# Gated linear attention and routed experts: first step in halves, decay rows turned as they land, sums of tiles 9 and 10 in two parts

## The chip, the cores and the metric

The kernel runs on one core of a Trainium2 chip. The core has TensorE for matrix products (PE; its weight loads are listed apart as PEld), VectorE (DVE), ScalarE (ACT) and GpSimd (POOL) for element work, and SyncE (SP), which here only issues transfers. ACT and POOL issue transfers of their own. The metric is the time of one execution in device microseconds.

## What is computed

A recurrent attention runs over 4 batches, 8 heads and 768 positions, with head dimension 48; its result, as 3072 rows of 384 numbers, goes through a layer of 8 experts, each row through the one expert that its gate prefers.

```python
for t in range(S):
    state = alpha[:, :, t, :, None] * state + einsum('bhd,bhe->bhde', k[:, :, t], v[:, :, t])
    y[:, :, t] = einsum('bhd,bhde->bhe', q[:, :, t], state)
x = y.transpose(0, 2, 1, 3).reshape(B * S, H * D)
logits = x @ w_gate                       # 3072 x 8
e = argmax(logits); gate_w = softmax(logits)[e]
out = gate_w * (relu(x @ w1[e]) @ w2[e])  # w1: 384 x 1024, w2: 1024 x 384
```

## The kernel before

The positions are cut into 6 chunks of 128, and a tile is one chunk of one batch: tile s is chunk c = s // 4 of batch b = s % 4, 24 tiles in all, chunk by chunk. Within a tile the recurrence becomes matrix products. The logarithms of alpha are summed over the positions by a product with a triangular matrix; the exponentials of the sum and of its negative (cp and icp) scale q and k; the scaled q and k are turned with the positions in columns, multiplied with each other (scores), masked by the triangle and multiplied with v. What earlier chunks left is a state for each head. It is scaled by a decay factor at each new chunk, and read by the scaled q.

One loop, over i from -4 to 23, does a step for each tile, with all stages shifted against each other. I call it step i. The order in which a step emits its operations is written out by hand (the pool of instructions is not reordered, L387), and so it is the order in each engine's queue. In step i:

- SP issues loads (`loads_for`, L629). Up to step 2 these are one tile of 192 KB each, in the order that the table `singly` (L623) spells out: "aakq" are two tiles of alpha, one of k and one of q. Later they go two tiles at a time.
- PE does the scores of tile i (L502), the turns of tile i+1 (L489), a sum (L430 or L433) of a tile up to five ahead, the reads of the state (L529, from tile 4 on), the products with v (`attend`, L539), in steps 0 to 2 a second sum, the products of keys and values for the state (`keys_values`, L550), and the rows of tile i-1 with their gate logits (L576).
- ACT copies y of tile i-1 out of its bank (yT, L558), takes an exponential for the gate (L590), the logarithm of alpha for the tiles whose sum is next (lna, L413), copies kT (L495), takes icp and cp (L436, L437), scales the finished rows (xs, L601) and issues the decay rows (L450).
- DVE applies the masks (dA, dB, L510), adds to the state (acc, L566 and L568), copies qT (L493, in early tiles also kT), and makes the gate weights.
- POOL makes the scaled k and q of tile i+2 (`operands`, L479) and the decayed state U (`scale_state`, L517), and in between prepares the routing.

A sum of tile s < APART = 11 is one product of f32 operands (L430). From tile 11 on the logarithm is split: hi is the logarithm times 512 in f16 (L418, on ACT), lo is the rest in a reduced f32 form (L423, on DVE), and the sum is two products (L432, L433). The hi and lo parts are made one step ahead of the sum. All sums use the PSUM bank "cum"; in steps below 0 the second sum uses the bank "x". In each step the sum waits until icp and cp of the sum before have read the bank.

The decay factor between two chunks of one batch is a product of three rows of 384: the last row of cp of the earlier chunk, the first row of icp of the later one, and alpha of the later one's first position. `decay_out` (L440) sends the first two as transfers from ACT's queue into a tile "dec" with one partition for each batch, and fetches alpha's rows for all four batches by one transfer from SP. `decay_rows` (L455) multiplies the three on POOL into "er", with every head padded from 48 to 64. `decay_cols` (L467) turns er by PE, four turns with 4 columns each, and copies the result to "E", which `scale_state` reads. decay_cols stands in steps 4, 8, 12, 16 and 20, behind the scores and ahead of the masks.

Ahead of the loop, `idle` (L637) issues three products on zeros from er, which DVE has set (L644). The layer of experts follows behind the loop. It is not touched.

## Time and profile before

| | us |
|---|---|
| median of three runs | 393.21 (391.83 to 393.31) |
| the profiled execution | 390.48 |
| its span, first to last instruction | 388.8 |
| attention loop, start to last mask | 0 to 133 |
| scores of step 0 start (PE's timeline) | 8.95 |
| scores of steps 1, 2, 3, 4, 5, 6 start | 14.08, 20.20, 26.07, 31.27, 37.05, 42.49 |
| granted TensorE clock, mean | 0.998 of full |
| transfers on queue q1 (SP's) | 57.77 MB, 63.2% of the transfer engines' time |
| transfers on queue q10 (ACT's) | 0.08 MB, 0.3% |

The profile is one execution. A line of a timeline holds the start in us, the duration in us, the engine, the line of the kernel, the operation, what it writes and reads, its shape and how many such operations were merged; in brackets stands how long the engine was idle before it and what it then waited for. ACTq and SPq are the issues of transfers in ACT's and SP's queue. In a list of waits, a line says which engine and line waited for which, the total in us, how often, and the longest wait. The durations of products on PE overlap one another, so from the start of one group to the start of the next is what a group costs.

### The profile page before, as it was taken

The page shows a single profiled execution, that of the slowest core. Times are in us where ns is not written, and L with a number is a line of the kernel's source. Part 1 is how long each engine was busy: PE and PEld are TensorE (multiplying, and loading weights), DVE is VectorE, ACT ScalarE, POOL GpSimd, SP SyncE. Part 2 cuts the span into 40 slices and gives each one's busy share as a digit, 9 for nine tenths or more (in the row PEclk, how much of TensorE's full clock was granted, in tenths as well). Part 3 has the DMA queues.
Part 4 walks back from the last instruction along what each step waited for, and adds up shares of the span by engine and source line. Part 5 has one row for each costly group of instructions (what it writes and reads, how often), then busy time and mean ns, then how long its engine had stood idle before and what let it go on. Part 6 is the DMA issues. An engine that isn't in the chain of part 4 may idle for free. (4 is left out here: it accounts for less than half of the span.)

```text
span 388.8 us, 9126 instructions
## 1 busy us (share of the span) xinstructions
PE 380.0 (98%) x3394; PEld 326.1 (84%) x3394; DVE 210.4 (54%) x649; ACT 230.2 (59%) x521; POOL 149.7 (39%) x203
## 2 busy tenths in 40 slices
PE   7999999999999999999999999999999999999995
PEld 4678888888888886899889979979979979979964
DVE  5554667676676666625843672582581582551200
ACT  4575777677665431545665775675765765763640
POOL 6557464789768203257050034025016012011032
PEclk9999999999999999999999999999999999999999
DMA  9999998998994315789959459758767966701211
GB/s 172 197 205 218 194 227 190 210 220 212 237 260 139 117 42 183 157 293 256 278 154 256 78 194 231 159 187 193 196 195 178 205 195 152 176 16 58 57 55 66
DMA packets 156546, 68.09 MB, mean 175 GB/s; under 512 B 139339, under 2 KB 150722, under 8 KB 156500
## 3 DMA queue, kind: packets, MB, share of 16 engines
q1 hardware_dynamic: 151396, 57.77, 63.2%
q0 software_dynamic: 3408, 9.64, 8.2%
q8 instruction: 28, 0.46, 0.5%
q10 hardware_dynamic: 1696, 0.08, 0.3%
q14 instruction: 18, 0.15, 0.1%
HBM read 49.00 MB, written 9.58 MB: 151 GB/s over the span
## 5 line engine op out<-in xcount | busy, mean ns | idle before, releaser
L1077 POOL DMA_INDIRECT out_dram<-zo,sp x25 | 26.0, 1041 | 136.5 <-ACT zo L1102 127.1
L479 POOL TENSOR_TENSOR kqb<-k_sb,icp 128x384 f32<-128x384 f32 x23 | 23.0, 1000 | 28.7 <-PE y L550 12.5
L1051 PE MATMUL tp<-h_sb,w 128*128 128x416 f32 (+5 forms) x96 | 33.9, 496 | 0.0
L502 PE MATMUL sA<-qT,kT 48*128 48x128 f32 x192 | 27.7, 284 | 0.9 <-DVE qT L493 0.9
L502 PE MATMUL sB<-qT,kT 48*128 48x128 f32 x192 | 27.7, 285 | 0.0
L372 POOL DMA_INDIRECT xg<-x_rows,gp x25 | 23.8, 953 | 10.0 <-issue 6.6
L489 PE MATMUL tp<-ident,kqb 128*128 128x128 f32 x192 | 26.4, 280 | 0.3 <-DVE kqb L479 0.3
L1051 PEld LDWEIGHTS tp<-h_sb,w 128*128 128x128 f32 x96 | 18.0, 190 | 10.3 <-issue 3.7
L502 PEld LDWEIGHTS sA<-qT,kT 48*128 48x128 f32 x192 | 23.1, 187 | 3.8 <-issue 1.1
L980 ACT ACTIVATE h_sb<-h_sb 128x208 f32<-128x208 f32 (+6 forms) x28 | 10.3, 366 | 25.3 <-DVE h_sb L192 24.5
L192 DVE TENSOR_TENSOR h_sb<-cum,u 128x208 f32<-128x208 f32 (+6 forms) x28 | 10.1, 360 | 27.2 <-PE cum L969 20.7
L479 POOL TENSOR_TENSOR kqb<-q_sb,cp 128x384 f32<-128x384 f32 x23 | 23.1, 1003 | 3.1 <-DMA q_sb<-in_q_dram 3.1
L192 DVE TENSOR_TENSOR h_sb<-sB,u 128x208 f32<-128x208 f32 (+6 forms) x28 | 10.1, 360 | 26.1 <-PE sB L969 18.7
L558 ACT COPY yT<-y 128x512 f32<-128x512 f32 x24 | 14.1, 586 | 16.5 <-PE y L550 9.1
L489 PEld LDWEIGHTS tp<-ident,kqb 128*128 128x128 f32 x192 | 20.5, 141 | 3.4 <-issue 0.8
L969 PE MATMUL tp<-xgT,w 128*128 128x208 f32 (+6 forms) x112 | 23.1, 329 | 0.0
L502 PEld LDWEIGHTS sB<-qT,kT 48*128 48x128 f32 x192 | 23.1, 187 | 0.0
L510 DVE TENSOR_TENSOR dA<-sA,cmask 128x512 f32<-128x512 f32 x24 | 16.5, 688 | 10.8 <-PE sB L502 10.6
L195 DVE TENSOR_TENSOR th<-h_sb,th 128x208 f32<-128x208 f32 (+5 forms) x48 | 17.3, 361 | 8.0 <-ACT h_sb L982 8.0
L881 ACT COPY xgT<-xt 128x768 uint16<-128x768 uint16 (+6 forms) x25 | 20.8, 922 | 0.5 <-DMA xt<-xh 0.5
L576 PE MATMUL x<-iw,yT 128*64 128x104 f32 x368 | 20.8, 255 | 0.1
L1102 ACT COPY zo<-zr 128x768 uint16<-128x768 uint16 (+2 forms) x20 | 19.9, 1052 | 0.0
(304 smaller groups left out, 1032.2 us busy)
## 6 DMA issues: line engine op xcount, KB each, us to landing
w<-in_moe_w_dram SPq DMA_DIRECT2D x14, 1536.0 KB, 7.9
x_rows<-xs SPq DMA_DIRECT2D x24, 192.0 KB, 3.7
v_sb<-in_v_dram SPq DMA_DIRECT2D x10, 384.0 KB, 4.8
k_sb<-in_k_dram SPq DMA_DIRECT2D x9, 384.0 KB, 6.3
q_sb<-in_q_dram SPq DMA_DIRECT2D x9, 384.0 KB, 5.9
a_sb<-in_alpha_dram SPq DMA_DIRECT2D x7, 384.0 KB, 4.3
a_sb<-in_alpha_dram SPq DMA_DIRECT2D x10, 192.0 KB, 3.7
w<-in_moe_w_dram SPq DMA_DIRECT2D x6, 256.0 KB, 3.7
```

What stands on the lines that cost most here:

```text
L192: eng.tensor_tensor(out, a, b, op=ALU.add)
L195: eng.tensor_tensor(out, a, b, op=ALU.subtract)
L372: nc.gpsimd.indirect_dma_start(out=g["xg"][:r, j, :], out_offset=None, in_=x_d[:, :], in_offset=bass.IndirectOffsetOnAxis(ap=g["gi"](j, r) ...
L479: eng.tensor_tensor(by_half(kq[:, i]), d[n].rearrange("s (a p) d -> s a p d", a=2), d[e][:].rearrange("s (a p d) -> s a p d", a=2, p=NP), ...
L489: nc.tensor.transpose(tp[:, p, :], pair(kqb[s % 3][:, i], p), ident[:])
L502: nc.tensor.matmul(t[:, p, :], lhsT=d["kT"][r : r + D, p, :], rhs=d["qT"][r : r + D, p, :], start=True, stop=True,)
L576: nc.tensor.matmul(d["x"][o : o + HC, m, : D2 + E], lhsT=d["yT"][:, m // 2, m % 2, o : o + HC], rhs=iw[:, m, :], start=True, stop=True,)
L881: nc.scalar.copy(to[:, :, :, j * C : j * C + r], g["xt"][:, j].rearrange("p (h a) t -> p h a t", h=2)[:, :, :, :r],)
L969: nc.tensor.matmul(out, lhsT=ops[n_][0], rhs=ops[n_][1], start=first and n_ == names[0], stop=True, skip_group_check=True,)
L1051: nc.tensor.matmul(d2[:, :n], lhsT=w2[:, f, 2 * C :], rhs=h[:, f, :n], start=(f == 0), stop=(f == FB - 1),)
L1077: ins = nc.gpsimd.indirect_dma_start(out=out[:, :], out_offset=bass.IndirectOffsetOnAxis(ap=g["si"](j, r), axis=0), in_=zo[:r], in_offset= ...
L1102: copy(zo[:r].bitcast(U16).rearrange("p (c h) -> p h c", h=2), g["zr"][:r, j].rearrange("p (h a) c -> p h (a c)", h=2),)
```

## The change

Four things are changed.

- *First step.* A function `first_step`, in step -2, replaces the sums of tiles 0 and 1, the operands of tile 0 (before on DVE in step -2) and its turns (before in step -1). The sum of tile 0 is made in two halves of two head pairs, in two banks; exponentials, operands, turns and copies go by halves. The sum of tile 1 stands between. In step 0 `keys_values` comes ahead of the second sum and no longer behind it. Two idle products of 512 columns on a constant zero stand ahead of everything, where three of 256 stood behind the first constants. In step -2 the load of v comes between the two of alpha.
- *Decay rows.* Three tiles "ends" of 20 partitions, filled with ones by POOL in step -4, take the rows as they are: for each chunk four rows of first positions of cp, four of last positions, four of alpha of the next chunk's first position (chunk 1 also those of chunk 0). Every head lands padded to 64. cp is stored with the heads in pairs, so that a row needs no other order. First and last row of a tile go in one transfer from ACT; alpha's rows go in two transfers from SP, and are asked for one chunk earlier. `decay_cols` turns all rows of the tile, takes the inverse of the first rows on the turned columns (the first row of cp in place of that of icp), multiplies it with what the chunk before handed on, and makes the product of last row and alpha to hand on.
- *Sums.* APART goes from 11 to 9, so tiles 9 and 10 are summed in two parts, and their logarithm and hi part are made one step earlier.
- `er`, `alpha0`, `decay_rows` and the "dec" tiles go.

```diff
@@ -65,7 +65,7 @@
     HC = C // 2
 
 
-    APART, HS = 11, 512.0
+    APART, HS = 9, 512.0
     assert NB * C == S and FB * C == F and DB * C == Dm and D <= DP
 
 
@@ -390,8 +390,8 @@
          tc.tile_pool(name="work", bufs=2) as work:
         st = {s: {} for s in range(NT)}
         y = ps.tile([C, 2, 512], F32, name="y")
-        er = work.tile([C, NP, 2, DP], F32, name="er", bufs=1)
-        decay, alpha0 = {}, {}
+        ends = [work.tile([5 * B, H, DP], F32, name=f"ends{i}", bufs=1) for i in range(3)]
+        decay, handed = {}, {}
 
         def yv(g):
             return y[:, g, : 2 * C].rearrange("r (j t) -> r j t", j=2)
@@ -424,8 +424,8 @@
                 t[:], in0=st[s]["hi"][:], scalar=-1.0 / HS, in1=st[s]["lna"][:], op0=ALU.mult, op1=ALU.add,
             )
 
-        def cums(s, bank="cum"):
-            cum = ps.tile([C, 512], F32, name="cum", tag=bank)
+        def cums(s):
+            cum = ps.tile([C, 512], F32, name="cum")
             if s < APART:
                 nc.tensor.matmul(cum[:, :Dm], lhsT=cum_m[:], rhs=st[s]["lna"][:], start=True, stop=True)
             else:
@@ -434,29 +434,32 @@
             cp = work.tile([C, Dm], F32, name="cp", bufs=6)
             icp = work.tile([C, Dm], F32, name="icp", bufs=6)
             nc.scalar.activation(icp[:], cum[:, :Dm], AF.Exp, scale=-1.0)
-            nc.scalar.activation(cp[:], cum[:, :Dm], AF.Exp)
+            nc.scalar.activation(by_pairs(cp), by_heads(cum[:, :Dm]), AF.Exp)
             st[s]["cp"], st[s]["icp"] = cp, icp
 
-        def decay_out(s, which=(0, 1)):
+        def decay_out(s):
+
+
             c, b = cb(s)
-            cp, icp = st[s]["cp"], st[s]["icp"]
-
-
-            for j in which:
-                cc, row = ((c, icp[0:1, :]), (c + 1, cp[C - 1 :, :]))[j]
-                if 0 < cc < NB:
-                    if cc not in decay:
-                        decay[cc] = work.tile([B, 2, Dm], F32, name="dec", bufs=3)
-                    nc.scalar.dma_start(decay[cc][b : b + 1, 1 - j, :], row)
-            if b == 0 and c + 1 < NB and 1 in which:
-                alpha0[c + 1] = work.tile([B, H, D], F32, name="alpha0", bufs=3)
-                nc.sync.dma_start(alpha0[c + 1][:], alpha[:, :, (c + 1) * C, :])
-
-        def decay_rows(c):
-            t = by_half(er[:B])
-            d = decay[c].rearrange("b i (a p d) -> b i a p d", a=2, p=NP)
-            nc.gpsimd.tensor_tensor(t, d[:, 0], d[:, 1], op=ALU.mult)
-            nc.gpsimd.tensor_tensor(t, t, alpha0[c].rearrange("b (a p) d -> b a p d", a=2), op=ALU.mult)
+            t = ends[max(c, 1) % 3]
+            first, last, alphas = (0, B, 2 * B) if c else (None, 3 * B, 4 * B)
+            if b == 0 and c + 1 < NB:
+                for a in range(2):
+                    nc.sync.dma_start(t[alphas : alphas + B, a::2, :D], alpha[:, a * NP : (a + 1) * NP, (c + 1) * C, :])
+            cp = st[s]["cp"].rearrange("s (h d) -> s h d", h=H)
+            if c == 0:
+                to, row = t[last + b : last + b + 1], cp[C - 1 :]
+            elif c + 1 < NB:
+                to, row = t[b : last + b + 1 : B], cp[:: C - 1]
+            else:
+                to, row = t[b : b + 1], cp[:1]
+            nc.scalar.dma_start(to[:, :, :D], row)
+
+        def by_heads(t):
+            return t.rearrange("s (a p d) -> s a p d", a=2, p=NP)
+
+        def by_pairs(t):
+            return t.rearrange("s (p a d) -> s a p d", a=2, p=NP)
 
         def by_half(t):
             return t.rearrange("s p a d -> s a p d")[:, :, :, :D]
@@ -465,21 +468,30 @@
             return t[:, p].rearrange("s a d -> s (a d)")
 
         def decay_cols(c):
+
+
+            n = 5 * B if c == 1 else 3 * B if c + 1 < NB else B
             ep = ps.tile([C, NP, C], F32, name="ep", tag="cum")
             for p in range(NP):
-                nc.tensor.transpose(ep[:, p, :B], pair(er[:B], p), ident[:B, :B])
+                nc.tensor.transpose(ep[:, p, :n], ends[c % 3][:n, 2 * p : 2 * p + 2, :].rearrange("r a d -> r (a d)"), ident[:n, :n])
             decay[c] = work.tile([C, NP, B], F32, name="E", bufs=2)
-            nc.vector.tensor_copy(decay[c][:], ep[:, :, :B])
+            nc.vector.reciprocal(decay[c][:], ep[:, :, :B])
+            if c == 1:
+                hand_on(c - 1, ep[:, :, 3 * B : n])
+            nc.vector.tensor_tensor(decay[c][:], decay[c][:], handed[c - 1][:], op=ALU.mult)
+            if c + 1 < NB:
+                hand_on(c, ep[:, :, B:n])
+
+        def hand_on(c, ep):
+            t = handed[c] = work.tile([C, NP, B], F32, name="handed", bufs=2)
+            nc.vector.tensor_copy(t[:], ep[:, :, :B])
+            nc.vector.tensor_tensor(t[:], t[:], ep[:, :, B : 2 * B], op=ALU.mult)
 
         def operands(s):
             d = st[s]
             kq = kqb[s % 3]
-            eng = nc.gpsimd if s else nc.vector
-            for i, n, e in ((0, "k", "icp"), (1, "q", "cp")):
-                eng.tensor_tensor(
-                    by_half(kq[:, i]), d[n].rearrange("s (a p) d -> s a p d", a=2),
-                    d[e][:].rearrange("s (a p d) -> s a p d", a=2, p=NP), op=ALU.mult,
-                )
+            for i, n, e in (0, "k", by_heads(d["icp"])), (1, "q", by_pairs(d["cp"])):
+                nc.gpsimd.tensor_tensor(by_half(kq[:, i]), d[n].rearrange("s (a p) d -> s a p d", a=2), e, op=ALU.mult)
 
         def transposes(s):
             d = st[s]
@@ -489,7 +501,7 @@
                     nc.tensor.transpose(tp[:, p, :], pair(kqb[s % 3][:, i], p), ident[:])
                 d[n] = work.tile([C, NP, C], F32, name=n)
 
-                if 0 < s < B - 1 or i and s < NT - B - 2:
+                if s < B - 1 or i and s < NT - B - 2:
                     nc.vector.tensor_copy(d[n][:], tp[:])
                 else:
                     nc.scalar.copy(d[n][:], tp[:])
@@ -620,7 +632,7 @@
 
         loaded = dict(a=0, k=0, q=0, v=0)
 
-        singly = {-5: "aakq", -4: "kqav", -3: "akq", -2: "aav", -1: "kq", 0: "avakq", 1: "avkq", 2: "a"}
+        singly = {-5: "aakq", -4: "kqav", -3: "akq", -2: "ava", -1: "kq", 0: "avakq", 1: "avkq", 2: "a"}
 
         def load_next(n, many):
             load(loaded[n], n, many)
@@ -636,12 +648,56 @@
 
         def idle(n):
 
-            t = ps.tile([C, NP, C], F32, name="sA")
+            t = ps.tile([C, NP * C], F32, name="sA")
+            z = nc.const_aps.tensor(0.0, (C, NP * C))
             for _ in range(n):
-                nc.tensor.matmul(t[:, :2, :], lhsT=er[:, 0].rearrange("s a d -> s (a d)"), rhs=er[:, :2], start=True, stop=True)
+                nc.tensor.matmul(t[:], lhsT=z[:, :C], rhs=z, start=True, stop=True)
+
+        def first_step():
+
+            d = st[0]
+            two = (slice(0, 2), slice(2, NP))
+
+            def heads(t, h):
+                return t.rearrange("s (a p d) -> s a p d", a=2, p=NP)[:, :, two[h]]
+
+
+            cum = [ps.tile([C, 512], F32, name=n)[:, : Dm // 2] for n in ("cum", "sB")]
+            for h in range(2):
+                nc.tensor.matmul(cum[h], lhsT=cum_m[:], rhs=heads(d["lna"][:], h), start=True, stop=True)
+            one = ps.tile([C, 512], F32, name="x")[:, :Dm]
+            nc.tensor.matmul(one, lhsT=cum_m[:], rhs=st[1]["lna"][:], start=True, stop=True)
+            icp, cp = (work.tile([C, Dm], F32, name=n, bufs=6) for n in ("icp", "cp"))
+            by = [icp.rearrange("s (h w) -> s h w", h=2)[:, h] for h in range(2)], [by_pairs(cp)[:, :, two[h]] for h in range(2)]
+            for t, f in zip(by, (-1.0, 1.0)):
+                for h in range(2):
+                    nc.scalar.activation(t[h], cum[h] if f < 0 else cum[h].rearrange("s (a p d) -> s a p d", a=2, p=2), AF.Exp, scale=f)
+            d["icp"], d["cp"] = icp, cp
+            by[0][:] = [t.rearrange("s (a p d) -> s a p d", a=2, p=2) for t in by[0]]
+            tps = []
+            for i, n in enumerate("kq"):
+                t = d[n + "T"] = work.tile([C, NP, C], F32, name=n + "T")
+                for h in range(2):
+                    if i and h:
+                        tp = ps.tile([C, NP, C], F32, name="cum")
+                    elif h == 0:
+                        tp = ps.tile([C, NP, C], F32, name="tp", bufs=2)
+                    tps.append((t[:, two[h]], tp[:, two[h]], nc.vector.tensor_copy if i else nc.scalar.copy))
+                    nc.vector.tensor_tensor(
+                        by_half(kqb[0][:, i])[:, :, two[h]], d[n].rearrange("s (a p) d -> s a p d", a=2)[:, :, two[h]],
+                        by[i][h], op=ALU.mult,
+                    )
+                    for p in range(2 * h, 2 * h + 2):
+                        nc.tensor.transpose(tp[:, p, :], pair(kqb[0][:, i], p), ident[:])
+            st[1]["icp"] = work.tile([C, Dm], F32, name="icp", bufs=6)
+            st[1]["cp"] = work.tile([C, Dm], F32, name="cp", bufs=6)
+            nc.scalar.activation(st[1]["icp"][:], one, AF.Exp, scale=-1.0)
+            for t, tp, copy in tps:
+                copy(t, tp)
+            nc.scalar.activation(by_pairs(st[1]["cp"]), by_heads(one), AF.Exp)
 
         loads_for(-5)
-        nc.vector.memset(er[:], 0.0)
+        idle(2)
         nc.gpsimd.memset(iw[:], 0.0)
         for i in range(2):
             nc.scalar.dma_start(
@@ -649,7 +705,6 @@
             )
         nc.vector.memset(y[:], 0.0)
         first_consts()
-        idle(3)
 
         eg = dict(apart=True)
         eg["h"] = early.tile([C, FB, EARLY], F32, name="h0")
@@ -728,13 +783,14 @@
             do(mask, i, 1)
             if i < B:
                 do(add_state, i - 1)
-            do(transposes, i + 1)
+            if i >= 0:
+                do(transposes, i + 1)
             sums = list(new_sums(i))
-            for s in sums[:1]:
-                cums(s)
-            if i < 0:
-                for s in sums[1:]:
-                    cums(s, "x")
+            if i == -2:
+                first_step()
+            else:
+                for s in sums[:1]:
+                    cums(s)
             do(gate_weight, i - 2)
             route(i)
             for s in new_logs(i):
@@ -746,20 +802,16 @@
             if i == -1:
                 for s in range(2):
                     decay_out(s)
-
-            if B - 1 <= i < 2 * B - 1:
-                decay_out(i + 1, (1,))
             if i == NT - 2:
                 si = next(se)[1]
                 eg["si"] = lambda j, r: si[:r, j : j + 1]
             if i in (B, 2 * B):
                 scale_state(i)
-            do(operands, i + 2)
+            if i > -2:
+                do(operands, i + 2)
             if i > 2 * B and i % B == 0:
                 scale_state(i)
-            if 0 < i + 1 < NT and (i + 1) % B == 0:
-                decay_rows((i + 1) // B)
-            elif i >= 0:
+            if i >= 0 and (i + 1) % B:
                 do(scale_state, i + 1)
             one_hots(nc.gpsimd, *on_gpsimd.get(i, ()))
             do(read_state, i)
@@ -770,11 +822,14 @@
                 early_turn(1)
             if i == NT - 2:
                 result(i)
+            if i == 0:
+                keys_values(i)
             if i >= 0 and sums[1:]:
                 cums(sums[1])
                 for s in sums:
-                    decay_out(s, (0,) if i else (0, 1))
-            do(keys_values, i)
+                    decay_out(s)
+            if i:
+                do(keys_values, i)
             if i == NT - 3:
                 held["tok"] = ps.tile([C, NC], F32, name="tok", tag="cum")
                 tokens(held["tok"][:], *range((NG - 1) * TG))
@@ -790,6 +845,9 @@
             if i in (-4, 0, 1):
                 for j in {-4: (0, 1, 2), 0: (3,), 1: (4,)}[i]:
                     late_consts(j)
+            if i == -4:
+                for t in ends:
+                    nc.gpsimd.memset(t[:], 1.0)
             if 12 <= i < 22:
                 fetch_part(groups[0], i - 12)
```

## The prediction

> **What bounds the kernel now.** I began with the head of the page: the span and the busy share of each engine.
>
> ```profile
> span 388.8 us, 9126 instructions
> PE 380.0 (98%) x3394; PEld 326.1 (84%) x3394; DVE 210.4 (54%) x649; ACT 230.2 (59%) x521; POOL 149.7 (39%) x203
> ```
>
> TensorE (PE) is busy nearly all the time, so an edit counts if it takes time from PE's own list or ends a wait of PE. Second came PE's timeline, two neighbouring steps with the two forms of the sum:
>
> ```profile
> 39.07 0.81 PE L430 MATMUL cum<-lna,cum_m 128*128 128x384 f32 x2
> 39.81 0.66 PE L529 MATMUL y<-qT,U 48*48 48x128 f32 x16
> ...
> 44.52 0.33 PE L432 MATMUL cum<-hi,cum_h 128*128 128x384 f16 x1
> 44.95 0.33 PE L529 MATMUL y<-qT,U 48*48 48x128 f32 x4
> ```
>
> From the sum to what follows it are 0.74 us in step 5 (tile 10, one f32 product) and 0.43 us in step 6 (tile 11, two parts). Nothing lies between: from step 4 on PE runs on without a gap. I call this stage PE-bound. Steps 0 to 3 are not quite. Third, therefore, ScalarE (ACT) at the start, and what PE waits for there:
>
> ```profile
> 11.30 0.52 ACT L413 ACTIVATE lna<-a_sb 128x384 f32<-128x384 f32 x1 [1.18 <-DMA a_sb<-in_alpha_dram]
> 11.81 0.49 ACT L436 ACTIVATE icp<-cum 128x384 f32<-128x384 f32 x1
> ...
> 14.59 0.51 ACTq L450 DMA_DIRECT2D dec<-cp  x1
> 15.19 0.59 ACT L558 COPY yT<-y 128x512 f32<-128x512 f32 x1 [0.63 <-ACT cp L437]
> ```
>
> ```profile
> 16.25 0.30 PEld L430 LDWEIGHTS cum<-lna,cum_m 128*128 128x128 f32 x2 [0.23 <-ACT lna L413]
> ```
>
> This is a chain that begins with a transfer: alpha of tile 3 lands at 11.3, its logarithm holds ACT until 11.82, then icp and cp of tile 2 (to 12.68), the sum of tile 3 on PE (12.74, it needs the bank that cp has read), icp and cp of tile 3 (to 14.56), the issue of a decay row (to 15.10), yT, the logarithm of tile 4, and the sum of tile 4 at 16.25, for which PE waited 0.23. Fourth, ACT in step 3 and SP's queue before it:
>
> ```profile
> 27.86 0.59 ACT L495 COPY kT<-tp 128x512 f32<-128x512 f32 x1 [0.26 <-PE tp L489]
> ...
> 29.77 0.58 ACT L601 ACTIVATE xs<-x,gw 128x384 f32<-128x384 f32 x1
> ```
>
> ```profile
> 14.58 0.86 SPq L453 DMA_DIRECT2D alpha<-in_alpha_dram  x1
> ...
> 24.05 2.06 SPq L405 DMA_DIRECT2D a_sb<-in_alpha_dram  x2
> ```
>
> xs ends at 30.35 and the rows of tile 2 (L576) start at 30.40; they need the bank that xs reads, so step 3 ends as ACT lets it. The first issue at 24.05 is alpha of tile 9. Last, the waits of PE's weight loads, and VectorE (DVE) where the decay factors are made:
>
> ```profile
> PEld y L529 <- POOL U L517: 1.4, 5, 0.5
> PEld ep L470 <- POOL er L459: 0.3, 1, 0.3
> PEld x L576 <- ACT xs L601: 0.2, 1, 0.2
> ```
>
> ```profile
> 32.80 0.17 DVE L472 COPY E<-ep 128x16 f32<-128x16 f32 x1
> 32.90 0.68 DVE L510 TENSOR_TENSOR dA<-sA,cmask 128x512 f32<-128x512 f32 x1
> ```
>
> **The change part by part, against the profiled run (390.48 us, of which the span is 388.8).**
>
> *Sums of tiles 9 and 10 in two parts.* Each saves PE 0.74 - 0.43 = 0.31 us; both steps are PE-bound: **-0.62**. Their hi and lo parts come in addition: ACT 0.52 and DVE 0.55 a tile. DVE is idle from 29.7 to 31.4 in step 3 and takes lo there, free. ACT is the matter of a later part.
>
> *Decay rows as they land.* The ten multiplications on GpSimd (POOL; L458, L459, 1.00 us each) go. They lie in POOL's idle time, except at step 8, where the scores take 1.26 us to the next group against 1.09 elsewhere, because ep waits for er: **-0.17**. The 40 row transfers on ACT become 24, at some 0.5 us of issue each; in steps 3 to 6 three become one. No wait of PE ends on these there, so I count nothing. The four turns at a chunk's start take 0.34 us with 4 columns, and a turn of 128 columns takes 0.93 / 8 = 0.116 us, so 20 columns in place of 4 add under 0.02 us in all.
>
> *More small DVE operations.* One copy becomes six at step 4 (inverse, copy, product, E's product, and two more), four at steps 8, 12, 16, and two at step 20. Queued behind them are the masks dA and dB; behind E wait U on POOL and then the reads of the state (L529). The trace gives two spacings: 0.10 us to the next operation that doesn't need the result (32.80 to 32.90), 0.21 to one that does (40.48 to 40.69, L255 to L256). At step 4: inverse 32.80, copy 32.90, product 33.11, E 33.32 to 33.49, U to 34.1. The reads are due at 34.37 - 0.31 = 34.06: **+0.15**. [...] At steps 8 to 16, E is 0.2 later and U ends some 0.3 before the reads; at step 20 up to 0.1 is lost, within the +0.15. The masks have about a microsecond of slack.
>
> *First step in halves, products for keys and values ahead of the second sum.* The ACT part can't start before 5.40, when the logarithm of tile 1 is through, and the q product not before q lands (it waited 0.32, to 6.80). After that: half a product (192 columns, some 0.36 in place of 0.56), two turns in place of four, half a copy (0.41 in place of 0.69). So the scores of step 0 start near 8.45 and not 8.95. With keys_values ahead of the sum, PE no longer stands for the bank, and the scores of step 1 start near 13.5 in place of 14.08. But the chain shown above begins with a landing and holds none of what was made shorter: tile 3 lands at 11.3 as before, and the sum of tile 4 starts at 16.25 as before. PE now waits 0.75 there, not 0.23. I count **0**; the bounds are +0.1 (alpha of tile 5 comes behind v, 0.9 later, at about 15.7, and is needed at 16.1) and -0.55, if the chain is not what holds. The two wider idle products (1024 columns in place of 768, started some 0.6 earlier) end by about 4.6, and ACT wants their successors at 5.40: nothing. The memsets of the row tiles (3 on POOL, about 0.45 like L645) fit into the 2.6 us that POOL waited before 7.77.
>
> *What comes a step earlier, and what is put before it.* The logarithm and hi part of tile 9 now stand in step 3 ahead of kT (27.86) in ACT's queue; kT, icp, cp, xs and the rows of tile 2 are behind them. Alpha of tile 9 was issued at 24.05 and such loads land 3.8 us later (median of this tile's transfers), at 27.8. Then ACT runs ln 27.8, hi 28.35, kT 28.8, icp, cp, xs to 30.55: rows at 30.6 in place of 30.4, 0.2 lost. But SP gets three more issues ahead of this load: the first step of each chunk is now fetched in two halves, and that of chunk 2 is asked for in step 1, no longer in step 3. What does one cost? Around 14.58, three loads took 3.87 us of SP time (13.88 to 17.75) where 0.9 each is usual: some 1.2 lost to one such issue, two row transfers from ACT among it. The load after it took only 0.39, so part is caught up, because the transfers themselves are the limit (the DMA row of the page reads 9 there). Low bound: 0.1 each, their bytes are few. High bound: 0.95 each, one whole slot of 0.86 and its gap. [...] I take 0.25 each, 0.75 in all, nearer to the row with the catching up: **+0.95** for step 3.
>
> Sum: -0.62 - 0.17 + 0.15 + 0.95 = **+0.3 us**, a span of 389.1 and a profiled run of 390.8. The profiled run was 2.7 below the median of the three runs (393.21), so I add the difference to the median: **393.5 us**. The three runs spread over 1.5 us; 0.5% (2.0 us) is about what a measurement of this kernel can tell from no change, and the sum is far inside. What is late next, if step 3 is not: PE itself.
>
> **The rivals.**
>
> *The gain at the start is kept.* For it: the scores of steps 0 and 1 do come earlier by 0.5. Against it: the landing at 11.3 and the 0.23 wait. If the chain gives way, 0.5 comes from the start; all waits of steps 0 to 3 together are some 1.4. With a punctual tile 9: -0.79 + 0.15 + 0.2 - 0.5 = -0.9, so 392.3; at the far end 391.2. Chance 0.15, of which about half the far end.
>
> *SP's small issues cost a slot each.* Place: SP's queue before alpha of tile 9, ACT's queue in step 3. Price: tile 9 is 2.9 late, step 3 loses 3.1, the sum is +2.5: 395.7, slower. The whole change turns to loss from a landing after 28.25 (0.64 is what the other parts leave, less the 0.2). For it: 0.86 for 6 KB; against it: the 0.39 right behind. Chance 0.17.
>
> *The row transfers are held in order.* All rows of a chunk go into one tile, interleaved. If each had to wait for the landing of the one before (3.6 us median), ACT's queue would stand, with kT and the sums behind it. ACT is idle for about 1.5 us of a 5.2 us step, so some 2 us in each of a dozen steps: 24 us, 417. The trace shows no such wait; chance 0.05.
>
> *As summed:* 0.58, by itself 392.6 to 394.5. The remaining 0.05 are small mishaps.
>
> **How the numbers follow.** Range: down to 392.0 for most of the first rival, up to 395.6 for tile 9 late by all but the whole price; left out are its far ends and the held rows. Faster by over 0.5% needs 2.0 us, only the first rival's far end: 0.08. Slower by over 0.5%: the second rival nearly whole and the third: 0.20. Within: 0.72.
>
> **What would show it.** Scores of step 0 at about 8.45 and of step 1 at 13.5, the sum of tile 4 still at 16.2 to 16.3; in step 3 ACT idle before ln of tile 9 with DMA as releaser, and the gap before the rows of tile 2 longer than 0.2; sums of tiles 9, 10 at 0.43; no wait of ep in step 8; a short wait for U in step 4. I am wrong if the sum of tile 4 moves up with the scores, if tile 9 lands before 27.8, or if ACT's row transfers show idle times behind each other.

## The result, and the profile after

The changed kernel takes 395.42 us (median of 6 runs, 394.08 to 396.18) beside 392.85 us for the kernel before (6 runs, 391.83 to 393.31): ratio 1.0066, 95% interval [1.0042, 1.0090]. That is slower by 2.6 us. The time lies inside the range of 392.0 to 395.6, near its upper end, but past the 0.5% that the likeliest case allowed. The profiled execution took 394.08 us. The head of its page:

```profile
span 392.2 us, 9122 instructions
PE 381.1 (97%) x3394; PEld 326.1 (83%) x3394; DVE 214.3 (55%) x668; ACT 231.7 (59%) x526; POOL 141.4 (36%) x196
```

PE's busy time grew by 1.1 us, the span by 3.4: PE waits. Where it waits is read from the starts of the scores, in a table made from PE's timeline. Each row gives a profile's starts minus those of the first profile of before, in us; the edited kernels of the next section stand below.

| start of scores of step | 0 | 2 | 3 | 4 | 6 | 9 | 13 | 17 | 21 | 23 |
|---|---|---|---|---|---|---|---|---|---|---|
| changed kernel | -0.21 | 0.19 | 0.19 | 1.52 | 1.55 | 1.78 | 2.20 | 2.61 | 2.84 | 2.85 |
| the same, second profile | -0.37 | 0.03 | 0.02 | 1.79 | 1.82 | 2.05 | 2.47 | 2.89 | 3.13 | 3.13 |
| before, second profile | 0.03 | 0.03 | 0.03 | 0.02 | 0.56 | 0.64 | 0.64 | 0.64 | 0.64 | 0.64 |
| e1, sums undone | -0.37 | 0.35 | 0.35 | 0.69 | 1.09 | 1.33 | 1.76 | 2.18 | 2.42 | 2.42 |
| e2, alpha rows behind | -0.37 | 0.03 | 0.03 | 0.24 | 0.28 | 0.52 | 0.94 | 1.39 | 1.62 | 1.62 |
| e3, weights first | -0.37 | 0.03 | 0.03 | 1.60 | 1.23 | 1.06 | 1.08 | 1.09 | 1.29 | 1.30 |
| e12, two moves | -0.38 | 0.02 | 0.02 | 1.95 | 4.42 | 4.25 | 4.27 | 4.26 | 4.47 | 4.46 |
| e13, three moves | -0.37 | 0.38 | 0.39 | 0.61 | 0.24 | 0.06 | 0.08 | 0.08 | 0.28 | 0.29 |

The changed kernel loses in two ways: once in step 3 (0.19 to 1.52), and a little at each first step of a chunk (4, 8, 12, 16, seen in the columns behind them). Step 3 is the place that the prediction named. ACT's timeline there with the rows of tile 2 on PE, then SP's issues, with alpha's two row loads now ahead of tile 9's:

```profile
27.59 0.51 ACT L413 ACTIVATE lna<-a_sb 128x384 f32<-128x384 f32 x1
29.07 0.52 ACT L413 ACTIVATE lna<-a_sb 128x384 f32<-128x384 f32 x1 [0.98 <-DMA a_sb<-in_alpha_dram]
...
31.28 0.59 ACT L613 ACTIVATE xs<-x,gw 128x384 f32<-128x384 f32 x1
...
31.93 0.93 PE L588 MATMUL x<-iw,yT 128*64 128x104 f32 x16 [1.42 <-ACT xs L613]
```

```profile
24.15 1.15 SPq L448 DMA_DIRECT2D ends<-in_alpha_dram  x2
25.40 1.02 SPq L405 DMA_DIRECT2D a_sb<-in_alpha_dram  x2
```

Alpha of tile 9 is asked for at 25.40 in place of 24.05; ACT waits 0.98 us for it with kT, icp, cp and xs in its queue. The list of waits shows what PE then waits for:

```profile
PEld x L588 <- ACT xs L613: 2.8, 5, 1.5
...
PEld y L541 <- POOL U L529: 1.3, 5, 0.4
```

There are five waits for xs: one of 1.5 us in step 3, and four more, in steps 4, 8, 12 and 16, that the prediction did not have. The timeline of step 4 tells what the four are:

```profile
34.34 0.26 DVE L478 RECIPROCAL E<-ep 128x16 f32<-128x16 f32 x1 [0.78 <-PE ep L476]
...
35.16 0.17 DVE L488 TENSOR_TENSOR handed<-handed,ep 128x16 f32<-128x16 f32 x1
...
35.38 0.10 PEld L432 LDWEIGHTS <-cum_h 128*128 128x128 f16 x1 [0.29 <-DVE handed L488]
...
36.44 0.68 DVE L505 COPY qT<-tp 128x512 f32<-128x512 f32 x1
37.04 0.14 DVE L606 TENSOR_SCALAR gw<-gw 128x1 f32<-128x1 f32 x1
37.21 0.16 DVE L607 RECIPROCAL gw<-gw 128x1 f32<-128x1 f32 x1
...
37.32 0.53 PE L562 MATMUL y<-v_sb,kqb 128*48 128x48 f32 x16
...
37.41 0.58 ACT L613 ACTIVATE xs<-x,gw 128x384 f32<-128x384 f32 x1 [0.55 <-DVE gw L607]
...
38.05 0.76 PE L588 MATMUL x<-iw,yT 128*64 128x104 f32 x12 [0.20 <-ACT xs L613]
```

The same two groups of PE in the kernel before:

```profile
35.86 0.53 PE L550 MATMUL y<-v_sb,kqb 128*48 128x48 f32 x16
36.22 0.90 PE L576 MATMUL x<-iw,yT 128*64 128x104 f32 x16
```

Six small operations stand on DVE, from 34.34 to 35.33; behind them come the masks, qT, and then the two operations of the gate weight, which end at 37.37. ACT stands 0.55 us for that weight before xs, and PE waits for xs before the rows: from the start of the products for keys and values to the start of the rows it is 0.73 us where it was 0.36. The line at 35.38 is a second wait of this chain: the sum of tile 9 needs the bank that the last of the six reads, and comes 1.15 us behind the turns where it came 0.93 behind.

The two-part sum of tile 10 does what it should: what follows it starts 0.43 us behind it. The first step is faster without use: its scores start at 8.74, and the sum of tile 4 is as late as ever.

```profile
40.93 0.33 PE L432 MATMUL cum<-hi,cum_h 128*128 128x384 f16 x1
...
41.36 0.66 PE L541 MATMUL y<-qT,U 48*48 48x128 f32 x16
```

```profile
16.45 0.91 PE L430 MATMUL cum<-lna,cum_m 128*128 128x384 f32 x2 [0.55 <-ACT lna L413]
```

Last, there is a wait of 0.71 us in the experts' part, at 177.12, which before does not have; a second profile of the same kernel (e11) does not have it either.

### The profile page after: what moved, and what is told of

It is laid out like the page before. It is cut to its first block, busy times and chain, and to the rows that moved or that the text cites. A ratio compares the mean times of both kernels' runs of the same rounds, so it can differ in the third digit from the quotient of the medians.

```text
span 392.2 us, 9122 instructions
## 1 busy us (share of the span) xinstructions
PE 381.1 (97%) x3394; PEld 326.1 (83%) x3394; DVE 214.3 (55%) x668; ACT 231.7 (59%) x526; POOL 141.4 (36%) x196
## 4 chain that ended last, share of the span: by engine, by line
PE 84%; ACT 4%; issue 4%; DVE 4%; DMA 3%; POOL 1%; ACTq 0%; POOLq 0%; DVEq 0%
PE tp L1109 8%; PE sA L1027 6%; PE x L1027 6%; PE sA L514 5%; PE y L551 5%; PE sB L1027 4%; PE cum L1027 4%; PE x L588 4%; PE tp L1027 4%; PE x L1092 4%; PE tp L501 4%; PE sA L1092 3%; PE tp L1092 2%; PE y L541 2%; PE cum L1092 2%
## 5 line engine op out<-in xcount | busy, mean ns | idle before, releaser
L501 PE MATMUL tp<-ident,kqb 128*128 128x128 f32 x184 | 25.1, 280 | 0.0
L494 POOL TENSOR_TENSOR kqb<-q_sb,cp 128x384 f32<-128x384 f32 x23 | 23.5, 1021 | 0.5 <-ACT cp L697 0.3
L501 PEld LDWEIGHTS tp<-ident,kqb 128*128 128x128 f32 x184 | 19.7, 140 | 2.3
```

The source lines that it names most:

```text
L494: nc.gpsimd.tensor_tensor(by_half(kq[:, i]), d[n].rearrange("s (a p) d -> s a p d", a=2), e, op=ALU.mult)
L501: nc.tensor.transpose(tp[:, p, :], pair(kqb[s % 3][:, i], p), ident[:])
```

## The experiments

Three groups of four kernels; each group ran on one chip beside the kernel before (medians 391.15, 392.67 and 391.47 us), and every ratio is to that.

**e1: the sums of tiles 9 and 10 whole again** (`APART, HS = 11, 512.0` in the changed kernel).

> Edit: the changed kernel with tiles 9 and 10 summed in one f32 product again. The changed kernel's trace has a hole of 1.95 us ahead of the rows of tile 2 in step 3 (0.62 before). Theory L (the landing of alpha of tile 9 holds ACT): with no logarithm of tile 9 in step 3 the hole goes back to about 0.6, steps 4 and 5 get 0.31 each back, and step 4 loses the small wait ahead of its sum (0.2): about 0.9 less than the changed kernel's 395.4, so 394.5, some 1.7 above the kernel before. Theory B (the chunk boundaries): the waits ahead of the rows in steps 4, 8, 12, 16 (0.73 where 0.36 is usual) stay as they are. Rival: if the hole in step 3 comes from the row transfers on ACT, it stays, and the time is 0.6 above the changed kernel's, 396.0.

392.68 us, ratio 1.0034 [1.0023, 1.0046]: not longer than the changed kernel (1.0066 and, in e11, 1.0052), but by its profile 0.4 to 0.7 us shorter; the intervals of the times overlap. The rows of tile 2 start 0.96 us behind the start of the products ahead of them, and not 1.95 (0.61 in before; the rest is not explained). Of the four later waits those in steps 8, 12 and 16 stay at 0.73; in step 4 it is gone (0.35), for there the whole sum, itself late for the bank, keeps PE back by as much. So the two-part sums, with tile 9 as late as it is here, cost more in step 3 than they save.

**e2: alpha's rows of chunk 2 behind tile 9's load.**

```
+        def alpha_rows(c): ...   # the two row loads
-            if b == 0 and c + 1 < NB:
-                for a in range(2): nc.sync.dma_start(...)
+            if b == 0 and c + 1 < NB and c != 1:
+                alpha_rows(c)
...
+            if i == 2:
+                alpha_rows(1)        # in loads_for, behind load_next
```

> Edit: the changed kernel, in which SP issues the two halves of alpha's rows for chunk 2 behind the load of tile 9's alpha and no longer ahead of it. Theory L (that the two issues in front of it make the load late): alpha of tile 9 is issued 1.2 us earlier and lands near 27.9, ACT waits for it 0.1 to 0.3 and not 0.98, the rows of tile 2 start 1.1 to 1.2 earlier: 394.2. Rival W (the additional work on ACT, a logarithm and a hi part of 1.0 us together, holds kT and xs, and not the landing): the hole ahead of the rows stays within 0.2 of 1.95, the time at 395.4.

393.61 us (392.16 to 396.8), ratio 1.0064 [1.0037, 1.0092]. By the time alone that is no gain; the profile shows the place mended. ACT's timeline:

```profile
27.40 0.93 ACT L413 ACTIVATE lna<-a_sb 128x384 f32<-128x384 f32 x2
28.35 0.52 ACT L418 ACTIVATE hi<-lna 128x384 f16<-128x384 f32 x1
```

Both logarithms run back to back, step 3 loses 0.21 in place of 1.33 to 1.76, and scores 23 start at +1.62. The run that the profile shows was 392.16 us, the shortest of the eight. Three runs took 392.2 to 392.3, four 393.5 to 394.0 and one 396.8: presumably the load is not punctual in each. This is taken up at e12. Counted from the scores of step 3 on, this profile loses 1.60 us and e1's 2.07: by these two profiles the two-part sums pay where the load is punctual.

**e3: the gate weight ahead of the decay factors at steps 4, 8, 12, 16, 20.**

```
             if 0 < i < NT and i % B == 0:
+                gate_weight(i - 2)
                 decay_cols(i // B)
...
-            do(gate_weight, i - 2)
+            if i <= 0 or i % B:
+                do(gate_weight, i - 2)
```

> Edit: the changed kernel, in which at a chunk's start DVE makes the gate weights (two operations of 0.15 us, which need nothing of the decay rows) ahead of the decay factors and no longer behind the masks and copies. Theory B: at a boundary the added small operations push the gate weights back, xs on ACT waits for them (0.55 idle), the rows on PE wait for xs. With the weights first the waits ahead of the rows in steps 4, 8, 12, 16 go (0.37 each, some 0.2 in step 20): 1.5 to 1.8 less, 393.7. Rival U (the boundaries lose on the state U, which comes later as E does, or on the longer issue of row transfers on ACT): the waits stay, the time is 395.4. The hole in step 3 is not touched by it under either.

391.85 us, ratio 1.0021 [1.0008, 1.0035]. The four waits are gone (0.36 us from products to rows at each), though not one operation less runs on DVE (668 in both). Step 4, ACT:

```profile
36.83 0.58 ACT L613 ACTIVATE xs<-x,gw 128x384 f32<-128x384 f32 x1
```

xs follows cp at once. Against the changed kernel each of these four boundaries gains 0.4 (step 8: -0.17 against +0.24; steps 12 and 16: 0.00 against +0.42), and the end of the ep wait, -0.17 at step 8, is now seen by itself. The wait for the bank at step 4 stays (0.30). So do 0.2 us at step 20, where no sum stands between the turns and the reads of the state: POOL is idle 0.53 us until E is ready, and the reads wait 0.37 us for U (0.17 in before).

**e4: the kernel before with the two-part sums alone** (`APART, HS = 9, 512.0` in before).

> Edit: the kernel before with only the sums of tiles 9 and 10 in two parts. Theory L: without the added issues on SP, alpha of tile 9 lands at 27.8 as before, ACT has the logarithm and hi part to do ahead of kT, the rows of tile 2 come 0.2 later than before, and steps 4 and 5 gain 0.31 each: 0.4 less than the kernel before, 392.4. Rival W (the added work on ACT holds step 3 whatever lands when): the hole in step 3 grows by 1.0 or more, as in the changed kernel, and the time is 0.4 to 0.7 above the kernel before, 393.3 to 393.5.

392.40 us, ratio 1.0034 [1.0019, 1.0050]. Neither expectation met it. Three row transfers a step still go out on ACT there, and the hi parts come in addition. ACT, from the end of step 5:

```profile
42.20 2.12 ACTq L450 DMA_DIRECT2D dec<-cp  x2
44.36 0.59 ACT L558 COPY yT<-y 128x512 f32<-128x512 f32 x1 [2.24 <-DMA dec<-cp]
```

Two issues take 2.12 us (1.19 at this place in before, 1.2 to 1.7 at its neighbours), yT stands behind them, and the rows start 0.99 us behind the products in steps 5 and 6, where 0.36 is usual. The changed kernel with its 24 row transfers loses nothing in these two steps. That points to a worth of fewer transfers, which the prediction put at nothing; no run has the changed kernel with 40, so this is argued and not shown.

**e6: the first step as it was**, in the changed kernel (whole sums and products, `keys_values` behind the sum, loads "aav").

> The changed kernel with its first step as it was: sums of tiles 0 and 1 whole, products of tile 0 in one piece each on VectorE, the sum of tile 3 ahead of the products for keys and values, loads in the old order; all else is the changed kernel. Theory S (the chain from the landing of tile 3's alpha holds the sum of tile 4, so the halves give nothing): scores of step 0 at 8.95 and of step 1 at 14.1, the sum of tile 4 at 16.3 to 16.5, and a time within 0.2 us of the changed kernel, that is a ratio to the kernel before of 1.006 to 1.0075. Rival (the halves do give their 0.3 to 0.5 us): the sum of tile 4 near 16.8 and a ratio of 1.0075 to 1.009.

395.35 us, ratio 1.0079 [1.0048, 1.0110]. The interval holds both expectations, and the sum of tile 4, at 16.71, lies between them too. This profile is 0.3 us late from the start (scores of step 0 at 9.28 and not 8.95, tile 3's logarithm at 11.53). Counted from the sum of tile 3, the sum of tile 4 starts 3.64 us later here, 3.52 and 3.51 in the two profiles of before, 3.58 and 3.57 in those of the changed kernel: with halves or without, that part of the chain is as long. By the time alone this trial decides nothing.

**e7: the logarithm of tile 4 first.** It stands behind cp of tile 3, ahead of yT and of the row transfers, which go out behind the second sum of step 1.

```
                 cums(sums[1])
-                for s in sums:
-                    decay_out(s)
+                if i == 0:
+                    logs(B)
+                else:
+                    for s in (2, 3, *sums):
+                        decay_out(s)
```

> The changed kernel with one link of the start chain moved: the logarithm of tile 4 stands on ScalarE right behind the exponentials of tile 3, ahead of the copy yT and of the two row transfers, and these two are issued with those of tiles 4 and 5 behind the second sum of step 1. Theory S: the sum of tile 4 starts when TensorE is through with the turns of tile 2, at 15.75 in place of 16.45, the scores of step 2 at 19.8 in place of 20.4, and 0.5 to 0.7 us stay to the end: ratio to the kernel before 1.005. Rival (behind this link another one is late at once, the logarithm of tile 5 or the bank that the exponentials of tile 4 free): scores of step 2 at 20.3 or later and a ratio of 1.0066 as the changed kernel.

396.54 us, ratio 1.0101 [1.0070, 1.0131]. The `else` holds in step 2 too, so the rows of tiles 2 and 3 are sent twice, and four transfers stand in line in both steps. That costs: scores of step 3 at +2.03. The time says nothing on the chain; the profile has the sum of tile 4 at 15.57 in place of 16.45.

**e8: e7, e2 and e3 together; e9: the same with whole sums.**

> The changed kernel with three moves of single instructions: the gate weights ahead of the decay factors on VectorE at steps 4, 8, 12, 16, 20 (profile of its own trial: 1.56 us less at the start of the last steps), the two loads of alpha rows of chunk 2 behind the load of tile 9 (1.23 less) and the logarithm of tile 4 first (0.6 less, if its own trial holds). If the three losses are separate places, they add: the last steps start 2.85 - 1.56 - 1.23 - 0.6 = -0.5 us against the kernel before, ratio 0.9985 (0.997 to 1.0005). If step 3's late rows come from ScalarE's queue being full and not from the landing alone, 0.3 to 0.5 us remain there: ratio 1.000.

> The same with the sums of tiles 9 and 10 whole again. If the two parts save TensorE 0.31 us each once tile 9 is punctual and the gate weights come first: 0.3 to 0.6 us longer than the kernel with the three moves. If the added logarithm and scaled copy in steps 3 and 4 cost ScalarE as much as TensorE gains: the same within 0.2 us. In either case the rows of tile 2 should start within 0.4 us of the end of the products before them, since no logarithm of tile 9 stands in step 3.

e8: 394.25 us, ratio 1.0046 [1.0030, 1.0062]; e9: 395.16 us, 1.0059 [1.0033, 1.0084]. Both hold e7's doubled rows and so decide nothing on the sums. e8 shows two things. Scores of step 2 start at 19.59, 0.61 ahead of before: with the logarithm of tile 4 ahead of yT and with tile 5's alpha on time, the start chain gives way. And ACT, right after:

```profile
19.25 3.31 ACTq L461 DMA_DIRECT2D ends<-cp  x3
22.66 0.59 ACT L575 COPY yT<-y 128x512 f32<-128x512 f32 x1 [3.32 <-DMA ends<-cp]
```

In the profiles of the changed kernel, e7, e8, e12 and e13 a row transfer issued by itself, from step 0 on, took 0.62 to 0.73 us of ACT's queue; the three last of four in line took 1.0 to 1.1 each here (3.31 and 2.92 for three), 0.7 to 0.8 in e7 (2.37 and 2.22).

**e10, e11: before and changed kernel once more.**

> The kernel before, unedited, for its second profile beside the runs below. Question: the wait of about 1.05 us in the experts' part (a product into sA, TensorE's start to start), which the profiles of the changed kernel and of the four trials of the start show and those of before and of the first four trials don't. If it is no work of the change, it can turn up here too. If it belongs to the changed kernel's program, it is absent here. Time: ratio 1.000; the scores of steps 0, 1, 2 within 0.2 us of 8.95, 14.1 and 20.2.

> The changed kernel, unedited, for its second profile beside the runs below. Ratio 1.0066 (1.004 to 1.009). If the wait of 1.05 us in the experts' part belongs to the program, it is here again; if to the single run, it is here or in the kernel before by chance. Whatever it does, the two places that the trials named stand: the rows of tile 2 about 2 us behind the products before them, and 0.73 us at steps 4, 8, 12 and 16.

e10: ratio 0.9990 [0.9979, 1.0000]. e11: 393.56 us, 1.0052 [1.0032, 1.0072]; rows of tile 2 at 2.38 us, the four boundaries at 0.73. The experts' wait is in neither profile. It was in the first profile of the changed kernel and in e6 to e9, so it comes and goes with the same program, and 0.7 of the first profile's 3.4 us are this wait. Neither the two profiles of the kernel before nor that of e4 has it; whether it can occur there is not shown. e10 also waits 0.46 for er at step 4 where the first profile did not: the wait that the change removes costs before up to 0.5 in some runs.

**e12: e3 and e2 together.**

> The changed kernel with the gate weights ahead of the decay factors at steps 4, 8, 12, 16, 20, and with the two loads of alpha rows of chunk 2 behind the load of tile 9. If the two losses are separate places, they add: 1.56 and 1.23 us less than the changed kernel, so that the last steps start within 0.3 us of the kernel before: ratio 1.000 (0.9985 to 1.0015). If one hides the other: ratio 1.002 to 1.0035.

392.37 us (390.54 to 395.38 in 22 runs), ratio 1.0040 [1.0020, 1.0060], a spread of 4.8 us. The profiled run was 395.11, and it shows why. Alpha of tile 9 was asked for at 24.12, 1.3 us earlier than in the changed kernel and with the small issues behind it, and ACT still waited for it until 29.50. PE's line for the rows of tile 2, and the stretches of PE's busy time and granted clock (the clock is the number after POOL's count):

```profile
32.35 0.94 PE L593 MATMUL x<-iw,yT 128*64 128x104 f32 x16 [2.01 <-ACT xs L618]
```

```profile
28.00:32.00 4.00, 2.33 (x37) 1.63 (x35) 2.22 (x6) 2.47 (x6) 0.15 (x1) 1.00 0.87 174
32.00:36.00 4.00, 3.65 (x38) 3.25 (x39) 1.15 (x7) 2.21 (x6) 0.00 (x0) 0.67 1.14 241
36.00:40.00 4.00, 4.00 (x34) 3.13 (x34) 3.31 (x10) 1.93 (x4) 3.22 (x4) 0.50 1.26 236
```

After the 2.01 us wait the clock is at half from about 33.3 to 40.2. Step 4 takes 8.57 us where e13 below takes 5.72: 2.85 us for one fall of the clock. In e11 PE waited 1.85 at the same place and the clock stayed at 1.00.

The mean granted clock of each run tells how often this happens. In 10 of the 22 runs it is 0.988 to 0.994, and they took 393.35 to 395.38 us; in the other 12 it is 0.996 to 1.000, and they took 390.54 to 392.50 us. The two runs of e3 at 395 us have 0.989 and the one of e2 at 396.8 has 0.991; none of the 43 runs of the kernel before in this group is below 0.997. That each fall had a wait in step 3 ahead of it is seen in the one profile only.

**e13: e12 with the logarithm of tile 4 first, as in e7, and the rows of tiles 2 and 3 sent once**, behind the exponentials of tile 4. The lines shown are set against e12.

```
+            if i == 1:
+                for s in (2, 3):
+                    decay_out(s)
             if i <= 0 or i % B:
                 do(gate_weight, i - 2)
...
                 cums(sums[1])
-                for s in sums:
-                    decay_out(s)
+                if i == 0:
+                    logs(B)
+                else:
+                    for s in sums:
+                        decay_out(s)
```

> The same with the logarithm of tile 4 ahead of yT on ScalarE, and the row transfers of tiles 2 and 3 behind the exponentials of tile 4 in step 1 (once; four of them in line held ScalarE for 2.4 to 3.3 us in the two trials before). If the start chain holds the sum of tile 4: scores of step 2 at 19.6 to 19.8 in place of 20.2 to 20.4, 0.5 us less than with the two moves: ratio 0.9987 (0.997 to 1.0005), the shortest of all. If the two row transfers or the second pair, closer together now, hold ScalarE ahead of the copy yT of step 2: scores of step 3 at 26.3 or later, and the ratio of the two moves or worse.

391.01 us, ratio 0.9988 [0.9977, 0.9999]: 2.55 us below the changed kernel of its group, and the only edited kernel below before. But by its profile it is not for the reason given. PE at the start:

```profile
15.57 0.81 PE L430 MATMUL cum<-lna,cum_m 128*128 128x384 f32 x2
...
18.51 0.91 PE L430 MATMUL cum<-lna,cum_m 128*128 128x384 f32 x2 [1.08 <-ACT cp L437]
```

The sum of tile 4 came up to 15.57, and the sum of tile 5 fell behind: alpha of tile 5 landed only at 17.18, and ACT has its logarithm ahead of icp and cp of tile 4. Scores of step 2 start at +0.38. What made this run short is e12's two moves with tile 9's alpha on time (asked for at 23.94, logarithms back to back at 27.76) and no fall of the clock. In all 14 runs the mean clock is 0.996 or more, against 12 of 22 in e12. The third move is all that differs between the two kernels; how it would keep tile 9 punctual is not shown.

## Why the prediction was right and wrong

| term | predicted | shown | by |
|---|---|---|---|
| sums of tiles 9, 10, PE alone | -0.62 | -0.31 in step 5; at step 4 the wait for the bank takes back 0.22 | profile after |
| ep wait, step 8 | -0.17 | -0.17, covered by the gate weight's wait in the changed kernel | e3 |
| more operations on DVE | +0.15 | +0.41 at four boundaries by the gate weight, 1.6; in addition 0.2 at step 4 for the bank and 0.2 at step 20 for U | e3 |
| first step | 0 | +0.19 and +0.03 at step 2 | profiles after, e11 |
| alpha of tile 9 late, step 3 | +0.95 | +1.33 and +1.76 in two profiles | e2 |

**The time is in the range in part by luck.** The upper end of the range stood for tile 9 late by nearly the whole price of three issues, 2.4 us above the 393.21 us from which the prediction started. Measured beside each other, the two kernels differ by 2.57 us (392.85 to 395.42). About half of that is step 3; most of the other half is a wait that the prediction put at nothing.

**Right: step 3, by place and chain; the size was low, and the cause of the late load is in part open.** ACT is idle for a DMA ahead of tile 9's logarithm, and the rows of tile 2 are late. With the load there in time, e2's rows of tile 2 start at 30.64, where the prediction had 30.6. For the size, the prediction took 0.25 us for each of three small issues. The first one, the second half at 15.17, was caught up by 23.5 (the q load ahead of the pair at 23.47 in place of 23.33). The pair directly ahead of tile 9's load was not: its 1.15 us and the gap stand whole between 24.15 and 25.40. That is 0.6 for each of two and nothing for the third. With the pair's start 0.1 later, tile 9 was asked for 1.35 later, where the prediction had 0.75. Here the issues right ahead of the load counted, and the one long before did not. But the place in SP's queue is not the whole cause: in e12 the load had the place that e2 gave it, and still landed at 29.50, later than the 29.07 of the changed kernel's first profile.

**Right in its result, for a part by another link: the start.** Scores 0 and 1 start earlier by 0.2 to 0.5 (8.58 to 8.74, 13.55 to 13.71), the sum of tile 4 starts at 16.28 to 16.45, and nothing is kept. From the sum of tile 3 on, the prediction's chain holds (e6), and moving one of its links moves the sum of tile 4 up to 15.57 (e7, e13). But the landing of tile 3, with which the prediction began the chain, is not what holds the sum of tile 3 each time. The kernel before, then the changed one:

```profile
12.20 0.48 ACT L437 ACTIVATE cp<-cum 128x384 f32<-128x384 f32 x1
12.74 0.91 PE L430 MATMUL cum<-lna,cum_m 128*128 128x384 f32 x2
```

```profile
12.00 0.48 ACT L437 ACTIVATE cp<-cum 128x384 f32<-128x384 f32 x1
12.41 0.53 PE L562 MATMUL y<-v_sb,kqb 128*48 128x48 f32 x16
12.87 0.91 PE L430 MATMUL cum<-lna,cum_m 128*128 128x384 f32 x2
```

In before the sum follows cp. In the changed kernel tile 3's logarithm is 0.17 earlier (11.13 in place of 11.30) and cp has read the bank at 12.48, but the sum starts at 12.87, behind the products for keys and values that the change puts ahead of it. So in this profile the new order gives away what the landing left. In the second profile cp ends at 12.65 and the sum starts at 12.71: there the order costs nothing. No run has this order alone. e13 adds that the next link can be a landing, tile 5's, which held the sum of tile 5 for 1.08 us; in the changed kernel that load was in time, as the prediction's bound of +0.1 has it.

**Wrong: "The masks have about a microsecond of slack", and with it most of the cost of the DVE term.** The working followed E to U to the reads, and the masks, and ended there; it did not read DVE's queue to its end within the step. There stands the gate weight, ACT's xs hangs on it, and PE's rows hang on xs. At step 8 of before the gate weight ends at 56.69 and xs starts at 56.73; from the end of xs to the rows it is 0.27 us (57.31 to 57.58). That is all the slack there is, and in the changed kernel the gate weight ends 0.60 later behind the turns (2.92 us after their start in place of 2.32). For steps 8 to 16 the prediction counted no loss, and it was 0.41 at each. The second thing it passed over is that ep lies in the bank of the sums, so each reader of ep stands before the next sum.

What the working did follow was right. It had E's product start 0.52 us behind the inverse (32.80 to 33.32), and so it is (34.34 to 34.86). The short wait for U at step 4 is there, 0.24, and hides behind the bank's; at step 20 the path from E over U to the reads costs 0.2, where the prediction allowed up to 0.1.

**Not borne out in sum: the two-part sums.** Their saving is real on PE, yet the profile of e1, without them, is shorter than the changed kernel's: they bring the logarithm of tile 9 into step 3, in front of kT and xs, and make PE wait for its load. With the load in time (e2's profile) they pay.

With the measured sizes the sum reads: +1.33 to 1.76 (step 3), +0.34 (step 4, with the saving of its sum), -0.31 (step 5), +0.24, 0.42, 0.42, 0.23 (steps 8, 12, 16, 20), start 0.0 to 0.2: 2.8 to 3.1 us in the profiles, 2.1 to 2.6 in the medians. The rival "SP's small issues cost a slot each" came nearest in time (395.7 against 395.42), but half of the loss had another cause. At its price of 0.95 a slot, two halves would cost 1.9 us; they took 1.25 us with the gap (24.15 to 25.40), where the one whole load of before took 0.97 (14.58 to 15.55).

Open: why tile 9's load lands 3.7 us after its issue in the changed kernel's profile and 5.4 in e12's, and why e13 keeps it in time; the experts' wait. Whether two-part sums pay with e13's moves was not measured, since e8 and e9 hold the doubled rows.

## What to carry to other kernels

When operations are put ahead on an engine, read that engine's queue to the end of the step and follow each thing behind them to PE; the victim here was the last and smallest, a 128x1 reciprocal. A tiny transfer can cost the load right behind it its whole issue time: here two of them took 1.25 us ahead of tile 9's load (24.15 to 25.40), while the one issued long before, at 15.17, was caught up by 23.5. Where an operation of one element per row releases a long one, place it first: e3's profile gained 1.6 us by order alone. And when the runs of one kernel spread, compare their granted clocks: e12's long runs, 393.35 us and more, have a mean of 0.988 to 0.994, its others 0.996 to 1.000.

## What the runs showed of the hardware

- One wait of PE of 2.01 us (e12, ahead of the rows at 32.35) was followed by 6.8 us at half clock (33.3 to 40.2; the mean clock is 0.67 from 32 to 36, 0.50 from 36 to 40, 0.98 from 40 to 44), 2.85 us of loss. In e8 a wait of 2.03, ahead of the sum at 32.16, was followed by 3.4 us of it (32.9 to 36.4; 0.62 from 32 to 36, 0.95 from 36 to 40). 1.85 us (e11) was not, nor was e8's 2.23 at 24.0, with 1.00 in both. In e12 PE was busy for 2.33 of the 4 us from 28 to 32, and in e11 for 2.34 without a fall. So waits of nearly the same length were followed by the fall in one place and not in another; what decides it is not shown.
- Row transfers on ACT: 0.50 to 0.59 us for a row issued by itself in before (0.90 the longest of two in line), 0.62 to 0.73 for a transfer of the changed kernel from step 0 on (also in e7, e8, e12, e13), with one padded row or two, 0.7 to 1.1 each for the last three of four in line (e7, e8).
- The same 192 KB load of tile 9 was there 3.7 us after its issue (the changed kernel, 25.40 to 29.07), 4.0 (e11, 25.35 to 29.34) and 5.4 (e12, 24.12 to 29.50), by the start of its logarithm.
- The first DVE operation on the turned columns, the inverse of 128x16, takes 0.26 us (the changed kernel, 34.34) where the copy of before took 0.17 (32.80). In step 4 of the changed kernel the copy behind the inverse, which does not need it, starts 0.17 us after it; behind that the small ones start 0.15 to 0.20 apart where one needs the one before, and one that does not starts after 0.10 (34.86 to 34.96).
